# Sparse attention and a routed mixture of experts: tokens placed in their expert's rows batch by batch, outputs added by DMA

## The chip, the cores and the metric

The kernel runs on one core of a Trainium2 chip (trn2). The metric is the device time of one execution in microseconds, as a median over runs. Engine names are those of the profile: PE multiplies matrices, DVE, ACT and POOL are the vector, scalar and GpSimd engines, SP issues most of the DMAs. Indirect DMAs, whose rows are chosen by an index in on-chip memory, are issued by POOL.

## The reference

An attention over 4 batches, 8 heads, 768 positions and a head dimension of 64 comes first. Of each row only the six most promising chunks of 32 keys are attended to. Its output, 3072 tokens of width 512, goes into a dense two-layer network and, for each token, into one of eight expert networks, the one with the highest gate value:

```python
x = attn_out.transpose(0, 2, 1, 3).reshape(B * S, H * D)      # 3072 x 512
y_dense = np.maximum(x @ w1_dense, 0.0) @ w2_dense            # 512 -> 512 -> 512
logits = x @ w_gate                                           # 8 experts
expert_idx = np.argmax(logits, axis=1)
gate_w = softmax(logits)[token, expert_idx]
y_moe[mask_e] = gate_w[mask_e] * (np.maximum(x[mask_e] @ w1[e], 0.0) @ w2[e])
out = y_dense + y_moe                                         # 3072 x 512, fp32
```

## The kernel before

**Attention stage.** The 16 pairs of heads run one after another, four pairs for each batch, each in 11 units (`NU`). A unit is a score matmul (L447), an exponential on ACT (L451), for some units a mask by POOL (`affine_select`, L453), and the product with the values (L466). The scores are issued two units ahead. The outputs of a batch are collected in `xbig`, a buffer for one batch, of which there are two. Preparations of later pairs (casts on POOL, transposes, chunk bounds on DVE) are laid among the units.

**Fills.** When a batch's attention is done, `batch_fills(b)` gives a list of closures that are laid among the units of the next batch: six transposes of the tokens (`xtr`), the gate (`gate`), the ranks (`ranks`, unit 9), and the dense network, of which `l1` computes hidden activations for three token tiles and `l2` one token tile of outputs. `ranks` counts, by matmuls with triangular and all-one matrices, the position of each token among those of its expert. `digits` writes a one-hot row for each token into `Am`. `gate` stores the tokens of the batch, with their gate weight, in two DRAM tables: `xo` (1056 bytes a row) and the right part of `xd` (3104 bytes a row). `l2` stores the dense outputs in the left part of `xd`.

**Tail.** After the attention, the fills of the last batch run by themselves. From the ranks of all batches a list of 31 blocks of 128 rows is built: each expert's tokens rounded up to whole blocks, and some blocks at the end that may be empty (24 token tiles give at most 24 + 7 blocks). The list is turned round by 24 matmuls (`pm`, L606) into `gi`, the token of every row of every block, and `si`, where its output goes; rows without a token get an index out of bounds and are not written.

**Blocks.** The loop over the 31 blocks is written out by hand, so that each engine finds work of the neighbouring blocks: in iteration i PE does the first layer of block i (`e1`), transposes the tokens of block i + 1 (`tx`), does the second layer of block i - 1 (`e2`) and transposes the hidden activations of block i (`th`). The weights' addresses come from registers (`offs`), loaded from the list. POOL gathers the rows of block i + 4 in one indirect DMA from `xd` (L646, buffer `xg`, six of them; the first four blocks take their tokens from `xo`). DVE multiplies the result by the gate weight and adds the dense outputs that came with the gather (L693), and POOL scatters the sum to `out` (L694).

The framework adds the semaphores, keeps each engine's instructions in an order near that of the program, and gives a buffer to its next user once all readers and writers of the last one are done. For a DMA that is when the data have landed.

Of the kernel before, what the change touches and what calls it, by code (L numbers as in the profile page):

```python
# [17 lines left out]
def kernel(  # L18
# [26 lines left out]
    RW = 2 * Dm + XW  # L45
# [5 lines left out]

    xd = dram.tile([N, RW], U16, name="xd")

    xo = dram.tile([N, XW], U16, name="xo")
    xov = xo.rearrange("(m p) w -> p m w", p=128)
    NX = 4
    xdv = xd.rearrange("(m p) w -> p m w", p=128)
# [10 lines left out]
    mx = ctx.enter_context(tc.tile_pool(name="mx", bufs=2))  # L68

# [78 lines left out]
    eone = const.tile([128, E], FP)  # L148
    relb = const.tile([128, NM], FP)
    Am = const.tile([128, NM, 128], HF)  # L150
    ones = const.tile([128, 128], HF)
    low = const.tile([128, 128], HF)
    io128 = const.tile([128, 128], HF)
    ioblk = const.tile([128, NBLK], HF)

    num = const.tile([128, NM], FP)
    xbig = [const.tile([128, NT, XW], HF, name=f"xbig{i}") for i in range(2)]

    def route_consts():
        for x2 in xbig:  # L160
            nc.gpsimd.memset(x2[:, :, Dm:XW], 0.0)
        nc.gpsimd.iota(iom8, pattern=[[0, NT], [1, E]], base=-E, channel_multiplier=0, allow_small_or_imprecise_dtypes=True)
        nc.gpsimd.memset(osum[:, 0], 0.0)
        nc.gpsimd.memset(eone, 1.0)
        nc.gpsimd.memset(ones, 1.0)
        nc.gpsimd.memset(low, 1.0)
        nc.gpsimd.affine_select(out=low, in_=low, compare_op=ALU.is_gt, fill=0.0,
                                base=0, pattern=[[1, 128]], channel_multiplier=-1)
        nc.gpsimd.iota(io128, pattern=[[1, 128]], base=0, channel_multiplier=0, allow_small_or_imprecise_dtypes=True)
        nc.gpsimd.iota(ioblk, pattern=[[1, NBLK]], base=0, channel_multiplier=0, allow_small_or_imprecise_dtypes=True)  # L170
        half = 2048 // 128
        nc.gpsimd.iota(num[:, 0:half], pattern=[[128, half]], base=-2048, channel_multiplier=1,
                       allow_small_or_imprecise_dtypes=True)
        nc.gpsimd.iota(num[:, half:], pattern=[[128, NM - half]], base=1, channel_multiplier=1,
                       allow_small_or_imprecise_dtypes=True)
# [57 lines left out]

    def batch_fills(b):
# [12 lines left out]
        def gate():  # L247
# [20 lines left out]
            for dst in (xov, xdv[:, :, 2 * Dm :]):  # L268
                nc.sync.dma_start(out=dst[:, b * NT : (b + 1) * NT], in_=xbig[b % 2].bitcast(U16))

        def rank():

            ohb = oh[:, b * NT : (b + 1) * NT]
            rk = ptile("rk", [128, NT + 1, E], FP, "rk")
            nc.tensor.matmul(rk[:, 0:NT], low, ohb, start=True, stop=False, skip_group_check=True)
            if b:
# [7 lines left out]
            ri = mg.tile([128, NT], mybir.dt.int32, name="ri")  # L284
            with nc.allow_low_precision("whole numbers below 2**24"):
                nc.vector.tensor_reduce(out=ri, in_=rt1, op=ALU.add, axis=mybir.AxisListType.X)
            r7 = mg.tile([128, NT], mybir.dt.int32, name="r7")
            nc.vector.tensor_single_scalar(r7, ri, 127, ALU.bitwise_and)
            rb = mg.tile([128, NT], mybir.dt.int32, name="rb")
            nc.vector.tensor_single_scalar(rb, ri, 7, ALU.arith_shift_right)  # L290
            rf = mg.tile([128, NT], FP, name="rf")
            nc.vector.tensor_copy(rf, r7)
            nc.vector.tensor_copy(relb[:, b * NT : (b + 1) * NT], rb)
            return rk, rf

        def digits(rf, t):
            m = b * NT + t
            nc.vector.tensor_scalar(Am[:, m], io128, rf[:, t : t + 1], num[:, m : m + 1], ALU.is_equal, ALU.mult)

        keep = {}  # L300

        def ranks():
            _, keep["rf"] = rank()
            ohb = oh[:, b * NT : (b + 1) * NT]
            with nc.allow_low_precision("whole numbers up to 24"):
                nc.vector.tensor_reduce(out=osum[:, b + 1], in_=ohb.rearrange("p t e -> p e t"), op=ALU.add,
                                        axis=mybir.AxisListType.X)
                nc.vector.tensor_add(osum[:, b + 1], osum[:, b + 1], osum[:, b])
# [14 lines left out]
        def l2(g, i, hold):  # L323
            def f():
# [7 lines left out]
                nc.sync.dma_start(out=xdv[:, m, 0 : 2 * Dm], in_=ys.bitcast(U16))  # L332
# [17 lines left out]
        for t in range(NT):  # L350
            at.setdefault(11 + 4 * t, []).append(lambda t=t: digits(keep["rf"], t))
# [3 lines left out]
        return out_list, dense, rank, digits, at  # L355
# [202 lines left out]
    with (  # L558
# [4 lines left out]
        tc.tile_pool(name="eg", bufs=6) as eg,  # L563
# [4 lines left out]
        a, d, rank, digits, _ = batch_fills(B - 1)  # L568
        for f in a:
            f()  # L570

        def dense(n):
            for _ in range(n):
                if d:
                    d.pop(0)()


        dense(2)
        rk, rf = rank()
        cnt = rk[:, NT]  # L580
        ni = const.tile([128, E], mybir.dt.int32)
        nc.vector.tensor_single_scalar(ni, cnt, 127.0, ALU.add)
        digits(rf, 0)
        nc.vector.tensor_single_scalar(ni, ni, 7, ALU.arith_shift_right)
        digits(rf, 1)
        be = const.tile([128, E], FP)
        nc.vector.tensor_tensor_scan(be, eone, ni, 0.0, ALU.mult, ALU.add)
        digits(rf, 2)
        bs = const.tile([128, E], FP)
        nc.vector.tensor_tensor(bs, be, ni, ALU.subtract)  # L590
        digits(rf, 3)
        tb = const.tile([128, NM, E], FP)
        nc.vector.tensor_tensor(tb, oh, bs.unsqueeze(1).to_broadcast([128, NM, E]), ALU.mult)
        digits(rf, 4)
        tbr = const.tile([128, NM], FP)
        nc.vector.tensor_reduce(out=tbr, in_=tb, op=ALU.add, axis=mybir.AxisListType.X)
        digits(rf, 5)
        bf = const.tile([128, NM], HF)
        nc.vector.tensor_add(bf, tbr, relb)
        eqb = const.tile([128, NM, NBLK], HF)  # L600
        nc.vector.tensor_tensor(eqb, ioblk.unsqueeze(1).to_broadcast([128, NM, NBLK]),
                                bf.unsqueeze(2).to_broadcast([128, NM, NBLK]), ALU.is_equal)
        dense(6)
        pm = p4.tile([128, NBLK], FP, name="pm")
        for m in range(NM):
            nc.tensor.matmul(pm, Am[:, m], eqb[:, m], start=(m == 0), stop=(m == NM - 1))  # L606
        up = const.tile([128, NBLK], FP)
        nc.vector.tensor_single_scalar(up, pm, 0.0, ALU.is_gt)
        gi = const.tile([128, NBLK], mybir.dt.int32)
        nc.vector.scalar_tensor_tensor(gi, pm, 2048.0, up, ALU.add, ALU.subtract)  # L610
        em = const.tile([128, NBLK], FP)
        nc.vector.tensor_scalar(em, pm, 0.0, 8192.0, ALU.is_equal, ALU.mult)
# [135 lines left out]
```

The softmax here doesn't subtract the row's maximum and nothing guards it: scores larger than these inputs give would overflow.

## Time and profile before

| | |
|---|---|
| time, median of 3 runs | 287.54 us (287.31 to 287.95) |
| time of the profiled execution | 306.61 us |
| its span in the profile | 304.9 us |
| mean granted PE clock over the span | 0.945 |
| PE busy | 241.6 us (79%) |
| DVE busy | 196.8 us (65%) |
| ACT busy | 174.4 us (57%) |
| POOL busy | 155.4 us (51%) |
| moved by DMA | 60.73 MB |

The profiled execution is slower than the others by 19 us, so durations read in it are compared with its own time. A share of busy time is a mean over stages that differ: attention until about 174.6 us of the span, then the last batch's fills, then the blocks. A busy PE is not a PE at its peak, since matmuls are pipelined and their clock can be reduced; the granted clock is listed by stage.

### The profile page before, as it was taken

To read this page: it belongs to the slowest core of one execution; us is meant where nothing else is said; L and a number is where in the kernel's file an instruction comes from. 1 tells how busy PE (TensorE), PEld (TensorE's weight loads), DVE (VectorE), ACT (ScalarE), POOL (GpSimd) and SP (SyncE) were. 2 spreads that over 40 slices of the span, in tenths; PEclk is the share of its full clock that TensorE was granted. 3 is DMA by queue.
4 is the path that set the end of the run, shared out by engine and by line. 5 is a ranking of instruction groups with operands and counts; after the bars stand their busy time and mean duration, and the time that the engine had idled before them with its cause. 6 is when DMAs were issued, how large, how long until landed. Compare 5 with 4: busy or idle time off the path is not lost.

```text
span 304.9 us, 7337 instructions
## 1 busy us (share of the span) xinstructions
PE 241.6 (79%) x2615; PEld 153.6 (50%) x2615; DVE 196.8 (65%) x620; ACT 174.4 (57%) x325; POOL 155.4 (51%) x203
## 2 busy tenths in 40 slices
PE   1179787789999888999899898838786697779691
PEld 1156566566667665667665554413443354335250
DVE  5479999999988999979996385122333233324141
ACT  3649788785979878789688633311333333234240
POOL 6566755553655636445412104473755566737432
PEclk9999999999999999999999999785999979959688
DMA  7999999999998999999972148685555755655510
GB/s 187 275 257 217 190 257 190 210 230 307 204 296 256 221 281 220 233 208 184 154 233 105 69 167 266 163 290 184 157 161 192 222 170 184 222 171 180 190 66 1
DMA packets 75636, 60.73 MB, mean 199 GB/s; under 512 B 28942, under 2 KB 68878, under 8 KB 75600
## 3 DMA queue, kind: packets, MB, share of 16 engines
q0 software_dynamic: 15184, 28.60, 40.5%
q1 hardware_dynamic: 60416, 31.66, 38.5%
q8 instruction: 21, 0.34, 0.4%
q14 instruction: 15, 0.12, 0.1%
HBM read 50.62 MB, written 20.91 MB: 235 GB/s over the span
## 4 chain that ended last, share of the span: by engine, by line
PE 40%; DVE 26%; ACT 11%; issue 10%; POOL 5%; DMA 5%; another core or an unknown queue 1%; POOLq 1%; ACTq 0%; SPq 0%; DVEq 0%
PE yp L690 8%; PE hp L673 7%; PE sp L447 5%; PE hp L318 4%; ACT ex L451 4%; DVE ks L389 4%; PE yp L327 4%; DVE m L426 3%; DMA xd<-ys 2%; POOL out_dram L694 2%; DVE rT L436 2%; DVE xbig L477 2%; PE tp L665 2%; PE tp L682 2%; PE op L466 2%
## 5 line engine op out<-in xcount | busy, mean ns | idle before, releaser
L451 ACT ACTIVATE ex<-sp 128x512 f16<-128x512 f32 (+1 forms) x176 | 90.0, 601 | 10.3 <-PE op L466 6.3
L447 PE MATMUL sp<-rT,kT 128*128 128x128 f16 (+3 forms) x384 | 63.9, 261 | 6.6 <-ACT ex L451 3.7
L453 POOL TENSOR_SCALAR_AFFINE_SELECT ex<-ex 128x512 f16<-128x512 f16 x48 | 32.7, 688 | 44.7 <-ACT ex L451 40.3
L694 POOL DMA_INDIRECT out_dram<-yo,si x31 | 31.4, 1013 | 37.0 <-DVE yo L693 32.2
L466 PE MATMUL op<-v,ex 128*128 128x65 f16 x672 | 45.7, 193 | 2.0 <-DVE xbig L477 1.0
L667 DVE COPY exT<-tp 128x512 f16<-128x512 f16 x31 | 13.1, 424 | 52.3 <-PE tp L665 24.7
L673 PE MATMUL hp<-we,exT 128*128 x124 | 37.1, 428 | 9.7 <-DVE exT L667 5.8
L684 ACT COPY ehT<-tp 128x512 f16<-128x512 f16 x31 | 18.1, 585 | 43.3 <-PE tp L682 29.9
L466 PEld LDWEIGHTS <-ex 128*128 128x128 f16 x672 | 35.5, 97 | 13.4 <-POOL ex L453 2.8
L690 PE MATMUL yp<-we,ehT 128*128 x124 | 36.8, 424 | 6.2 <-issue 3.7
L447 PEld LDWEIGHTS <-kT 128*128 128x128 f16 x384 | 29.8, 98 | 14.4 <-issue 9.2
L646 POOL DMA_INDIRECT xg<-xd,gi x31 | 29.8, 963 | 12.4 <-issue 7.6
L676 ACT ACTIVATE eh<-hp 128x512 f16<-128x512 f32 x31 | 18.5, 597 | 28.8 <-PE hp L673 14.9
L389 DVE TENSOR_REDUCE ks<-kp 128x24 f16<-128x768 f16 x32 | 29.3, 941 | 7.9 <-ACT kp L385 7.8
L693 DVE SCALAR_TENSOR_TENSOR yo<-yp,xg 128x512 f32<-128x512 f32 x27 | 20.2, 749 | 16.0 <-PE yp L690 10.0
L318 PE MATMUL hp<-xT,wd 128*128 128x384 f16 x128 | 26.1, 324 | 2.8 <-DVE rt L283 1.3
L327 PE MATMUL yp<-wd,hT 128*128 128x512 f16 x96 | 24.6, 378 | 0.7 <-DVE ys L224 0.3
L320 ACT ACTIVATE hT<-hp 128x384 f16<-128x384 f32 x32 | 15.7, 491 | 15.8 <-PE hp L318 12.7
L370 POOL CAST k<-kf 128x768 f16<-128x768 f32 x16 | 13.2, 824 | 19.6 <-PE pp L383 16.6
L673 PEld LDWEIGHTS <-exT 128*128 128x128 f16 x124 | 12.5, 108 | 20.5 <-issue 7.8
L690 PEld LDWEIGHTS <-ehT 128*128 128x128 f16 x124 | 12.3, 107 | 16.5 <-issue 7.4
L385 ACT COPY kp<-pp 128x768 f16<-128x768 f16 x16 | 12.9, 805 | 10.2 <-PE pp L383 10.2
(128 smaller groups left out, 422.8 us busy)
## 6 DMA issues: line engine op xcount, KB each, us to landing
we<-in_moe_w_dram POOLq DMA_DIRECT2D x16, 512.0 KB
kf<-in_k_dram SPq DMA_DIRECT2D x32, 192.0 KB, 4.6
qf<-in_q_dram SPq DMA_DIRECT2D x32, 192.0 KB, 4.5
vf<-in_v_dram SPq DMA_DIRECT2D x32, 192.0 KB, 7.4
xd<-ys SPq DMA_DIRECT2D x24, 256.0 KB, 4.0
xo<-xbig SPq DMA_DIRECT2D x4, 792.0 KB, 6.4
xd<-xbig SPq DMA_DIRECT2D x4, 792.0 KB, 8.4
wd<-in_moe_w_dense_dram POOLq DMA_DIRECT2D x2, 512.0 KB
```

The source lines that it names most:

```text
L318: nc.tensor.matmul(hp, wd[:, ko, j * 128 : (j + 1) * 128], xT[:, ko, g * G * 128 : (g + 1) * G * 128], start=(ko == 0), stop=(ko == NK - 1))
L327: nc.tensor.matmul(yp, hold["h"][:, j, i * 128 : (i + 1) * 128], wd[:, NK + j], start=(j == 0), stop=(j == NK - 1))
L389: nc.vector.tensor_reduce(out=ks[:, i], in_=kp.rearrange("d (c w) -> d c w", w=32), op=op, axis=mybir.AxisListType.X)
L447: nc.tensor.matmul(sp[:, o : o + w], kT[p % NB][g][:, kt * 128 : (kt + 1) * 128], rT[p % NB][g][:, a * 128 : z * 128], start=(o == 0), sto ...
L451: nc.scalar.activation(ex[:, 0:o], sp[:, 0:o], AF.Exp, scale=0.125)
L453: nc.gpsimd.affine_select(out=ex, in_=ex, compare_op=ALU.is_ge, fill=0.0, base=0, pattern=[[0, 4], [1, 2], [2, 64]], channel_multiplier=-1)
L466: nc.tensor.matmul(s["op", g][:, t * (D + 1) : (t + 1) * (D + 1)], ex[:, o : o + 128], v16[p % NB][:, g, kt, :], start=first, stop=(last_o ...
L646: nc.gpsimd.indirect_dma_start(out=dst, out_offset=None, in_=src, in_offset=bass.IndirectOffsetOnAxis(ap=gi[:, i : i + 1], axis=0))
L673: nc.tensor.matmul(hp, s["xT"][:, ko], wef[:, bass.ds(offs[i] + ko * 512, 512)], start=(ko == 0), stop=(ko == NK - 1))
L690: nc.tensor.matmul(yp, s["hT"][:, j], wef[:, bass.ds(offs[i] + (NK + j) * 512, 512)], start=(j == 0), stop=(j == NK - 1))
L693: nc.vector.scalar_tensor_tensor(o, yp, s["x"][:, Dm : Dm + 2].bitcast(FP), s["y"], ALU.mult, ALU.add)
L694: sc = nc.gpsimd.indirect_dma_start(out=out, out_offset=bass.IndirectOffsetOnAxis(ap=si[:, i : i + 1], axis=0), in_=o, in_offset=None, bou ...
```

## The change

The tables `xo` and `xd` go, and with them the one-hot digits, the list by matmuls, and all gathers. In their place:

- One DRAM table has room for all tokens in each expert's part (`CAP` = 3200 rows for each of eight experts) and one empty block at its end. Ranks now include the expert's first row (one more matmul, `ebase`), so that they are the row in the table (`slot`).
- `place(t)` scatters the 128 tokens of one tile to their rows by an indirect DMA. It is laid at units 12, 15, ... 27 of the next batch's attention. A token's row also carries its own number in `out` (32 bits next to the gate weight).
- `lists` is called twice: after batch 2 it lists the first 11 blocks (`N1`), those that are certain to be full of tokens of the batches 0 to 2, and after batch 3 the other 20 (`N2`). It writes the first row of each block (`ro`) and its weights' address (`eo`).
- `fetch(i)` loads a block's 128 rows by a plain DMA on SP, with the address in a register of SP. Five blocks are fetched ahead (`AHEAD`), in six buffers.
- The last batch's fills, its placing and the storing of empty rows behind each expert's last token (`empty`) are laid among the first ten blocks (`extra`). Blocks 0 to 10 are declared independent of the last batch's placing.
- The dense outputs are stored in `out` itself, each tile in two DMAs of 64 rows. In `e2` DVE only multiplies by the gate weight, and the scatter to `out` adds to what is there (`compute_op=ALU.add`). Its indices lie in the fetched rows, so the row's buffer is in use until that scatter is done.

```diff
-    xd = dram.tile([N, RW], U16, name="xd")
-    xo = dram.tile([N, XW], U16, name="xo")
+    CAP = N + 128
+    EMPTY = E * CAP
+    table = dram.tile([EMPTY + 128, XW], U16, name="table")
+    N1 = (N * (B - 1) // B - E * 127 + 127) // 128
+    N2 = NBLK - N1
+    outv = out.rearrange("(m p j) d -> m j p d", p=64, j=2)
...
-            for dst in (xov, xdv[:, :, 2 * Dm :]):
-                nc.sync.dma_start(out=dst[:, b * NT : (b + 1) * NT], in_=xbig[b % 2].bitcast(U16))
+            nc.gpsimd.tensor_copy(xbig[b % 2][:, :, Dm + 2 : Dm + 4].bitcast(mybir.dt.int32), num[:, b * NT : (b + 1) * NT])
...
+        def place(t):
+            def f():
+                sc = nc.gpsimd.indirect_dma_start(
+                    out=table, out_offset=bass.IndirectOffsetOnAxis(ap=keep["slot"][:, t : t + 1], axis=0),
+                    in_=xbig[b % 2][:, t].bitcast(U16), in_offset=None)
+                apart(sc, "rows", "every token has a row of its own")
+                if b == B - 1:
+                    tc.declare_no_dep(sc.ins, group="full", reason="the first blocks were full before this batch")
+            return f
...
-                nc.sync.dma_start(out=xdv[:, m, 0 : 2 * Dm], in_=ys.bitcast(U16))
+                for j in range(NJ):
+                    st_ = nc.sync.dma_start(out=outv[m, j], in_=ys[64 * j : 64 * j + 64])
...
-            at.setdefault(11 + 4 * t, []).append(lambda t=t: digits(keep["rf"], t))
+            at.setdefault(12 + 3 * t, []).append(place(t))
...
+        def fetch(i):
+            es[i]["x"] = xg = eg.tile([128, XW], U16, name="xg")
+            ld = nc.sync.dma_start(out=xg, in_=table[bass.ds(rows[i], 128)])
+            if i < N1:
+                tc.add_to_no_dep_group("full", ld.ins)
...
-            o = eg.tile([128, Dm], FP, name="yo")
-            nc.vector.scalar_tensor_tensor(o, yp, s["x"][:, Dm : Dm + 2].bitcast(FP), s["y"], ALU.mult, ALU.add)
-            sc = nc.gpsimd.indirect_dma_start(out=out, out_offset=bass.IndirectOffsetOnAxis(ap=si[:, i : i + 1], axis=0),
-                                         in_=o, in_offset=None, bounds_check=N - 1, oob_is_err=False)
+            o = et.tile([128, Dm], FP, name="yo", bufs=4)
+            nc.vector.tensor_scalar(o, yp, s["x"][:, Dm : Dm + 2].bitcast(FP), None, ALU.mult)
+            sc = nc.gpsimd.indirect_dma_start(
+                out=out, out_offset=bass.IndirectOffsetOnAxis(ap=s["x"][:, Dm + 2 : Dm + 4].bitcast(mybir.dt.int32), axis=0),
+                in_=o, in_offset=None, bounds_check=N - 1, oob_is_err=False, compute_op=ALU.add)
...
+        AHEAD = 5
+        load_rows(N1)
+        for i in range(AHEAD):
+            fetch(i)
+        load_offs(N1)
         tx(0)
+        extra = {0: a[:NT], 1: [a[NT], ranks], 2: places[:3], 3: places[3:], 4: [empty]}
+        for n, f in enumerate(d):
+            extra.setdefault(2 + n * (N1 - 3) // len(d), []).append(f)
         for i in range(NBLK):
+            if i + AHEAD == N1:
+                load_rows(NBLK)
+            if i + 1 == N1:
+                load_offs(NBLK)
+            if i + AHEAD < NBLK:
+                fetch(i + AHEAD)
             e1(i)
...
             if i + 1 < NBLK:
                 tx(i + 1)
+            for f in extra.get(i, ()):
+                f()
             if i > 0:
                 e2(i - 1)
             th(i)
```

## The prediction

> **What bounds the kernel now.** I read the busy table over time first, cut where the work changes: attention ends with the last use of its buffers at about 174.6 us, the routing of batch 3 follows, and from 189 us on the 31 expert blocks run. The columns are busy us (instructions) of PE, weight loads, DVE, ACT and POOL, then the granted clock, the DMA share and GB/s.
>
> ```profile
> 174.60:186.00 11.40, 10.76 (x115) 6.46 (x115) 10.04 (x46) 4.39 (x10) 0.00 (x0) 1.00 0.64 219
> 186.00:196.00 10.00, 8.00 (x42) 3.67 (x40) 2.08 (x5) 3.61 (x7) 5.41 (x6) 0.84 0.57 168
> 196.00:210.00 14.00, 7.88 (x42) 3.93 (x41) 3.01 (x5) 2.95 (x5) 8.80 (x10) 0.74 0.82 256
> 200.00:285.00 85.00, 63.33 (x382) 33.01 (x380) 27.14 (x47) 28.21 (x48) 50.73 (x52) 0.88 0.60 192
> 0.00:174.60 174.60, 143.35 (x1991) 102.38 (x1992) 150.30 (x512) 131.59 (x251) 90.28 (x137) 1.00 0.98 217
> ```
>
> Until 186 us PE is full. From 186 to 210 it is busy 15.9 of 24 us, much of it at a reduced clock. The chain of waits says why: the dense outputs must land in DRAM before a block's rows can be gathered from the same table.
>
> ```profile
> 184.79 3.47 DMA xd<-ys
> 189.77 3.68 DMA xd<-ys
> 199.21 5.15 DMA xg<-xd,gi
> ```
>
> Then the steady part. The costliest groups show two POOL instructions for each block, and the timeline shows how they follow one another:
>
> ```profile
> L694 POOL DMA_INDIRECT out_dram<-yo,si x31 | 31.4, 1013 | 37.0 <-DVE yo L693 32.2
> L646 POOL DMA_INDIRECT xg<-xd,gi x31 | 29.8, 963 | 12.4 <-issue 7.6
> ```
> ```profile
> 225.35 0.97 POOL L646 DMA_INDIRECT xg<-xd,gi  x1 [0.30 <-PE yp L690]
> 225.40 1.03 PE L673 MATMUL hp<-we,exT 128*128 x4
> 226.62 1.02 POOL L694 DMA_INDIRECT out_dram<-yo,si  x1 [0.30 <-issue]
> 227.57 1.03 PE L673 MATMUL hp<-we,exT 128*128 x4
> 227.94 0.97 POOL L646 DMA_INDIRECT xg<-xd,gi  x1 [0.30 <-issue]
> ```
>
> PE at full clock repeats every 2.17 us (225.40 to 227.57). POOL needs 0.97 + 0.30 + 1.02 + 0.30 = 2.59 us for a block. So **POOL is the slower of the two**, PE idles, and PE's clock falls. Measured: 25 scatters begin between 200 and 285 us, 3.4 us a block; PE is busy 63.3 of 85 us at a mean clock of 0.88.
>
> **What the Trainium skill says.** (1) "DMA: Bandwidth & Descriptors", section "SWDGE vs HWDGE vs iDMA": an accumulating DMA can only be issued from GpSimd. So the scatter stays on POOL; only the gather can leave. No accumulate is in this trace. (2) "Collectives: The Full Stack", section "The bandwidth ceiling": a reducing DMA is slower than a copy because it needs two source reads, about half the rate, not because of the addition. Not shown here either; I use a factor of 2. (3) The first page again, section "Two DMAs through the same engine are not ordered": of two read-modify-write packets directly after one another the second mostly read stale data. So such packets overlap in an engine, and a row isn't waited for before the next begins. (4) "TensorE: Matmul & The Clock Gate", section "What's actually happening": the clock halves after an idle window of some 3.4 us and returns after a busy one. The trace agrees: four L690 matmuls take 1.02 us at best, 1.91 us at 205 us, right after a PE idle of 4.5 us.
>
> **The change, part by part.** The profiled execution took 306.61 us (span 304.9, 1.7 around it), 19.1 us over the median of 287.54. I sum against the profiled one, then carry over.
>
> *Attention stage.* Off DVE: 18 digit masks at 312 ns (5.6 us), and 12 small casts and shifts at about 164 ns (2.0 us). Onto DVE: the first block list, 15 small instructions, some 11 at 0.17 and 4 at 0.3 us by the rows of be, ni, ge and ef: 3.1 us. Net -4.5 us on an engine busy 150.3 of 174.6 us, so part of it could shorten the stage. Onto POOL: 18 row scatters. The nearest row, L646, gives 0.97 + 0.30 us each, 22.9 us on an engine busy 90.3 of 174.6. They stand in POOL's order ahead of the mask selects that PE waits for:
>
> ```profile
> POOL ex L453 <- ACT ex L451: 40.3, 27, 7.4
> PEld L466 <- POOL ex L453: 2.8, 6, 1.0
> ```
>
> POOL waits 40.3 us for the exponentials, PE only 2.8 us for POOL, so most scatters find a gap. Bounds: -4.5 us (DVE all on the path) to +6 us (18 times a third of a microsecond lost behind a scatter; all of it lost is a rival). I take 0. SP issues 18 more stores (0.33 us each) and 6 big ones fewer; SP only waits here, and its waiting instructions hold back loads made two head pairs ahead, so nothing. One more rank matmul per batch (0.19 us): nothing.
>
> *Between attention and experts.* Gone: rank digits, the tb/eqb/pm chain, the 24 pm matmuls (0.76 us), the gathers xo and the wait for the dense stores. The first 11 blocks need only batches 0 to 2, whose rows were placed during attention; SP can fetch five of them ahead. PE work in this stage at full clock: 24 transposes (6 x 0.22 = 1.3), gate 0.8, ranks 0.4, eight L318 groups at 0.82 (6.6) and six L327 groups at 0.86 (5.2): 14.3 us. All of it now lies between expert blocks. Start (first transpose, its copy, register loads; the copy alone is 0.42 us, and PE waited 1.5 us at 190.97): 2 us.
>
> *Blocks.* PE 31 x 2.17 = 67.3 us. POOL falls to one instruction: 1.02 + 0.30 = 1.32 us, with 0.5 us more if three instead of two descriptors must be written; even 1.8 us is under 2.17. Six row scatters add 7.6 us once, in iterations that dense work stretches to about 3.6 us. SP takes the fetches, 0.33 us each: covered. The DVE output step loses an operand: nothing. The second list (16 small DVE instructions, about 3.4 us) stands ahead of a block's exT copy: I charge 2 us of PE.
>
> **The new wait** is in the fetch. A fetch needs the row buffer of the block six before it, which is free only when that block's accumulating scatter has landed. With T the time of a block: its e2 starts 1.08 us into the next iteration; from e2's start to the end of the scatter's instruction the last blocks took 3.08 us (294.40 to 297.48); a plain indirect transfer lands 1.85 us after its instruction (first xo gather: ends 187.19, PE has it at 189.04), with a doubled transfer I estimate 2 to 3; SP and the fetch's landing 2.5 (the shortest store landed in 2.0). That is 9.2 at the middle, and the rows are wanted 0.86 us into the iteration four later: 4T = 8.3, T = 2.1 us. Just inside 2.17, so I take PE's pace; each microsecond of landing more costs 0.25 us a block. Queued behind a waiting fetch on SP: dense stores (three ys buffers, whose copies on DVE and ACT would wait), the zero rows and the row registers. The dense stores come three at a time, some four iterations apart, and a fetch holds SP up for two to three: no charge.
>
> *End.* From the last e2's start to the end of the span:
>
> ```profile
> 298.54 1.02 PE L690 MATMUL yp<-we,ehT 128*128 x4 [0.82 <-ACT ehT L684]
> 300.63 0.98 POOL L694 DMA_INDIRECT out_dram<-yo,si  x1 [1.08 <-DVE yo L693]
> ```
>
> 304.9 - 298.5 - 0.9 for the group itself = 5.5 us, unchanged.
>
> **Sum.** Tail = 2 + 14.3 + 67.3 + 2 + 5.5 = 91 us against 130.3 in the profile. Of the 21.7 us in which PE stood idle between 200 and 285, several pauses stop ACT, DVE and PE together with no releaser shown; I leave 8 us of them. Profile: 174.6 + 91 + 8 + 1.7 = 275, 31 below 306.6. The unprofiled runs have at most 287.5 - 1.7 - 174.6 = 111 us of tail, so less to lose: 174.6 + 91 + 1.7 + 2 for clock and buffers = **269 us**, 18.5 below the median.
>
> **Rivals.** *Ring of row buffers* (0.22): an accumulating landing 2 us longer than assumed gives T = 2.6 to 2.7, as slow as POOL was; 20 blocks x 0.5 = 10, so 279 us. For it: the margin above is nil. *No overlap* (0.05): the first fetches still wait for batch 3; then the 8 us hole of 186 to 210 stays, 277 us. *Slower: the accumulate itself* (0.13). If rows of one engine are added one after another with a trip to DRAM each, eight rows an engine at 0.5 us are 4 us a block: 20 x 1.8 = 37 us more, 306. It turns the sign from T = 3.1 us on (269 + 20 x 0.93 = 287.5), which is a landing about 4 us longer than assumed. Against it: item (3). *Slower: placing during attention* (0.04): all 22.9 us of POOL on the path gives 292.
>
> **How the numbers follow.** PE's pace 0.56 (own range 260 to 275), ring 0.22, no overlap 0.05, the two slower cases 0.17. Faster by over 0.2% (about what measurement can tell from no change): 0.82; same 0.01; slower 0.17. The range 259 to 286 holds the faster cases and leaves out the slower.
>
> **What would show it.** Right: no idle of PE over 2 us between 175 and 200, e1 groups 2.2 us apart after block 11, one POOL instruction a block, clock 0.95 or more. Ring: PE or its loads wait for xg's DMA with SP behind the scatter. Accumulate: scatter packets several times the length of a copy. Placing: PE's wait for POOL selects well over 2.8 us, attention ending after 180. Attention ending before 170 would say DVE was the bound there and 269 too high.

## The result, and the profile after

The changed kernel takes **305.07 us** (median of 4 runs, 303.67 to 308.63) beside 287.43 us for the kernel before: a ratio of 1.060 (95% interval 1.054 to 1.066). In two later comparisons on two chips, each beside fresh runs of the kernel before, it was 1.041 (1.031 to 1.051) and 1.042 (1.028 to 1.056). Ratios here and below leave out executions more than 1.5% above the fastest of their kernel, so they can differ by up to 0.007 from the quotient of the medians. The forecast was 269 us; the change costs 12 to 18 us where it was to save 18.5.

The profiled execution took 304.44 us, its span is 302.7. The busy table over time of the changed kernel, cut as in the prediction (busy us (instructions) of PE, weight loads, DVE, ACT, POOL, then clock, DMA share, GB/s):

```profile
0.00:175.80 175.80, 141.59 (x1966) 102.58 (x1967) 143.05 (x495) 131.09 (x249) 108.59 (x163) 0.98 0.96 205
...
186.00:196.00 10.00, 9.62 (x97) 6.19 (x96) 7.36 (x31) 4.98 (x10) 3.80 (x4) 0.93 0.24 40
196.00:210.00 14.00, 9.36 (x59) 4.63 (x57) 4.49 (x7) 4.90 (x9) 9.90 (x8) 0.92 0.87 197
...
200.00:285.00 85.00, 62.52 (x387) 32.73 (x386) 26.97 (x46) 29.26 (x51) 37.40 (x25) 0.87 0.67 126
```

The last line is the one to compare: PE is busy 62.5 of 85 us, no more than before (63.3), although POOL fell from 50.7 to 37.4 us and is no bound any more. The profile of before was taken in an execution of 306.61 us; in one of 287.79 us (b_again, below) PE even reached 68.7:

```profile
200.00:285.00 85.00, 68.73 (x448) 34.82 (x447) 33.99 (x57) 33.10 (x56) 56.74 (x58) 0.90 0.63 208
```

Something else holds PE. The costliest groups show the parts as they were planned: one POOL instruction a block and 24 placing ones. The scatter, now adding, takes 1556 ns where the plain one took 1013:

```profile
L694 POOL DMA_INDIRECT out_dram<-yo,xg x31 | 48.2, 1556 | 69.8 <-DVE yo L693 51.6
...
L366 POOL DMA_INDIRECT table<-xbig,slot x24 | 23.5, 979 | 12.9 <-issue 5.8
...
L665 PE MATMUL tp<-ident,xg 128*128 128x128 f16 x124 | 13.0, 234 | 15.6 <-DMA xg<-table 15.6
```

The waits after 176 us (what waited, for what, us in total, times, longest) name two causes for PE and, in the SP queue, what stands behind the first:

```profile
PE tp L665 <- DMA xg<-table: 15.6, 5, 5.8
PE hp L673 <- issue: 6.9, 1, 6.9
```
```profile
SPq L657 <- DMA out_dram<-yo,xg: 77.4, 24, 16.4
SPq L762 <- DMA out_dram<-yo,xg: 12.2, 3, 8.4
SPq L641 <- DVE yo L693: 4.3, 1, 4.3
```

SP spends 77 us waiting to fetch a block's rows (L657) until an earlier block's scatter, which reads its indices from the same buffer, has landed. The other hole, 6.9 us in one piece, has no releaser. PE's timeline shows both kinds, three of the holes:

```profile
211.16 0.61 PE L665 MATMUL tp<-ident,xg 128*128 128x128 f16 x4 [5.79 <-DMA xg<-table]
...
235.18 1.44 PE L673 MATMUL hp<-we,exT 128*128 x3 [6.92 <-issue]
...
249.41 0.61 PE L665 MATMUL tp<-ident,xg 128*128 128x128 f16 x4 [2.87 <-DMA xg<-table]
```

The hole before 235.18 belongs to no data: in the trace PE's own queue runs one register load there, the 20 weight addresses of the second list, from 227.7 on for 7.28 us. It is the longer one of the two loads in this view of the list's tile (minimum, median and maximum in ns):

```profile
L641 PEldq TENSOR_LOAD <-eo x2: 1758/4521/7284, 179.4 to 227.7; - x2
```

In attention, the waits for POOL's masks, to be compared with 40.3 and 2.8 before:

```profile
POOL ex L521 <- ACT ex L519: 31.6, 25, 3.5
...
PEld L534 <- POOL ex L521: 8.1, 8, 2.5
```

The end of the span is as forecast: the last second-layer group starts at 296.31, and 302.7 - 296.3 - 0.9 = 5.5 us.

### The profile page after: what moved, and what is told of

The parts are those of the page before. It is cut to its first block, busy times and chain, and to the rows that moved or that the text cites. A ratio compares the mean times of both kernels' runs of the same rounds, so it can differ in the third digit from the quotient of the medians.

```text
span 302.7 us, 7430 instructions
## 1 busy us (share of the span) xinstructions
PE 236.5 (78%) x2595; PEld 153.8 (51%) x2595; DVE 188.8 (62%) x592; ACT 174.7 (58%) x325; POOL 162.6 (54%) x200
## 3 DMA queue, kind: packets, MB, share of 16 engines
q1 hardware_dynamic: 60288, 30.58, 40.2%
## 4 chain that ended last, share of the span: by engine, by line
PE 27%; issue 24%; POOL 22%; DVE 12%; ACT 10%; DMA 3%; POOLq 1%; SPq 0%; ACTq 0%; DVEq 0%
POOL out_dram L694 13%; PE sp L515 7%; ACT ex L519 4%; PE yp L391 4%; POOL table L366 4%; PE hp L382 4%; PE op L534 3%; PE pp L488 2%; DVE ks L457 2%; DVE m L494 2%; POOL ex L521 2%; PE pp L502 1%; PE tp L262 1%; PE hp L673 1%; DMA kf<-in_k_dram 1%
## 5 line engine op out<-in xcount | busy, mean ns | idle before, releaser
L519 ACT ACTIVATE ex<-sp 128x512 f16<-128x512 f32 (+1 forms) x176 | 91.1, 602 | 17.3 <-PE sp L515 10.7
L694 POOL DMA_INDIRECT out_dram<-yo,xg x31 | 48.2, 1556 | 69.8 <-DVE yo L693 51.6
L534 PEld LDWEIGHTS <-ex 128*128 128x128 f16 x672 | 36.2, 99 | 18.7 <-POOL ex L521 8.1
L673 PE MATMUL hp<-we,exT 128*128 x124 | 36.8, 420 | 9.3 <-issue 6.9
L693 DVE TENSOR_SCALAR yo<-yp,xg 128x512 f32<-128x512 f32 x31 | 23.2, 749 | 23.4 <-PE yp L690 23.3
L457 DVE TENSOR_REDUCE ks<-kp 128x24 f16<-128x768 f16 x32 | 29.2, 945 | 12.5 <-ACT kp L453 12.4
L690 PE MATMUL yp<-we,ehT 128*128 x124 | 34.7, 406 | 0.8 <-ACT ehT L684 0.8
L676 ACT ACTIVATE eh<-hp 128x512 f16<-128x512 f32 x31 | 18.5, 597 | 25.7 <-PE hp L673 25.4
L366 POOL DMA_INDIRECT table<-xbig,slot x24 | 23.5, 979 | 12.9 <-issue 5.8
L382 PE MATMUL hp<-xT,wd 128*128 128x384 f16 x128 | 27.7, 347 | 1.9 <-DVE rt L305 1.0
L665 PE MATMUL tp<-ident,xg 128*128 128x128 f16 x124 | 13.0, 234 | 15.6 <-DMA xg<-table 15.6
L665 PEld LDWEIGHTS <-xg 128*128 128x128 f16 x124 | 9.8, 105 | 24.5 <-DMA xg<-table 18.0
L673 PEld LDWEIGHTS <-exT 128*128 128x128 f16 x124 | 11.7, 105 | 17.8 <-issue 11.4
```

The source lines that it names most:

```text
L366: sc = nc.gpsimd.indirect_dma_start(out=table, out_offset=bass.IndirectOffsetOnAxis(ap=keep["slot"][:, t : t + 1], axis=0), in_=xbig[b % 2 ...
L382: nc.tensor.matmul(hp, wd[:, ko, j * 128 : (j + 1) * 128], xT[:, ko, g * G * 128 : (g + 1) * G * 128], start=(ko == 0), stop=(ko == NK - 1))
L457: nc.vector.tensor_reduce(out=ks[:, i], in_=kp.rearrange("d (c w) -> d c w", w=32), op=op, axis=mybir.AxisListType.X)
L519: nc.scalar.activation(ex[:, 0:o], sp[:, 0:o], AF.Exp, scale=0.125)
L534: nc.tensor.matmul(s["op", g][:, t * (D + 1) : (t + 1) * (D + 1)], ex[:, o : o + 128], v16[p % NB][:, g, kt, :], start=first, stop=(last_o ...
L673: nc.tensor.matmul(hp, s["xT"][:, ko], wef[:, bass.ds(offs[i] + ko * 512, 512)], start=(ko == 0), stop=(ko == NK - 1))
```

## The experiments

"Before" is the kernel before, run on the same chip beside them. Chips differ: the same kernel took about 287 us in the first comparison and on two chips after it, and 303 to 305 on two others. So only ratios are compared from one chip to another.

| run | edit to the changed kernel | us | before | ratio (95%) |
|---|---|---|---|---|
| b_again | (the kernel before) | 287.77 | 287.65 | 1.001 (0.999 to 1.004) |
| a_again | none | 299.54 | 287.65 | 1.041 (1.031 to 1.051) |
| e1_ring12 | 12 row buffers | 299.02 | 303.42 | 0.979 (0.970 to 0.988) |
| e2_plain | scatter without the add | 296.71 | 303.42 | 0.976 (0.969 to 0.983) |
| e3_offs4 | PE registers in fours | 302.58 | 303.42 | 0.993 (0.989 to 0.996) |
| g1_after | none | 318.95 | 304.87 | 1.042 (1.028 to 1.056) |
| g2_ring12 | 12 row buffers | 301.08 | 304.87 | 0.984 (0.975 to 0.994) |
| g3_offs4 | PE registers in fours | 308.04 | 304.87 | 1.006 (1.002 to 1.010) |
| g4_own_tile | 12 buffers, own tile for the PE list | 291.44 | 304.87 | 0.955 (0.947 to 0.962) |
| h1_shifted | the same, list 44 bytes into it | 281.99 | 286.32 | 0.985 (0.977 to 0.994) |
| c1_ring_offs | 12 buffers, PE registers in fours | 278.62 | 287.65 | 0.973 (0.966 to 0.979) |
| c2_parts | the same for SP too, 4 at the start | 276.12 | 287.22 | 0.964 (0.959 to 0.970) |
| h2_own_tiles | 12 buffers, own tiles for both lists | 272.95 | 286.32 | 0.950 (0.942 to 0.958) |
| f1_cut_noplace | ends after attention, no placing | 178.80 | 287.22 | |
| f2_cut_after | ends after attention | 183.54 | 287.22 | |
| f3_cut_before | the kernel before, ends there | 180.27 | 287.22 | |
| e4_cut_after | as f2 | 194.57 | 303.42 | |
| e5_cut_before | as f3 | 180.33 | 287.65 | |

**Theory**: the new wait in the fetch (six row buffers) and the register loads, both priced at next to nothing, hold PE. **Rivals**: the accumulate is slow by itself; the placing costs attention its gain.

### Both kernels again on one chip

b_again:

> The kernel before, unchanged, profiled beside the others on one chip. Its runs of the first comparison took 287 us and those of the second 303, so its trace is needed from the same chip as the experiments'. If chips differ in the attention stage alone: attention ends later than 172.6 us by as much as the whole is longer than 287. If the difference lies in the blocks: the tail after attention is longer instead.

a_again:

> The changed kernel, unchanged, on the same chip as the kernel before. If 6% is its true cost: about 1.06 times the kernel before. If the first comparison had the two on chips of different speed: between 0.99 and 1.02 times. Theory A (ring) expects the last 20 blocks to take 3 us each in either case.

Measured: 287.77 and 299.54 us. A profiled execution of the kernel before took 287.79 us here, so the profile itself costs nothing. In the first profiled one, of 306.61 us, attention's last product starts at 172.6 us as it does here; its 19 us more all lie behind that (132.3 us to the end of the span, 113.5 here). Whether a slower chip made them isn't shown: no trace of the kernel before was taken on one, and the changed kernel loses most of its time there in attention (last product at 189.1 us in g1_after, 175.8 in a_again). The blocks of b_again (first-layer groups, L673) follow at 2.54 us on the mean from the sixth on, (276.7 - 213.1)/25, close to POOL's 2.59 us as read in the prediction.

Attention's last product starts at 172.6 us in b_again and 175.8 in a_again; from there to the end of the span it is 113.5 and 121.1 us. So 3.2 us of the loss lie in attention and 7.6 after it.

### The ring of row buffers

Only the number of buffers, and only the add:

```diff
-    eg = ctx.enter_context(tc.tile_pool(name="eg", bufs=6))
+    eg = ctx.enter_context(tc.tile_pool(name="eg", bufs=12))
```

> One edit to the changed kernel: 12 row buffers (xg) instead of 6, still five fetched ahead. Theory A, the ring: the last 20 blocks take 3.1 us each because a fetch waits for the scatter six blocks earlier to land (4.5 to 5.4 us after its issue) and then lands itself only 4.4 us later. With 12 buffers neither wait is on the path; blocks go to about 2.2 us, 20 x 0.9 = 18 us less, some of the 5.8 us hole at 205 us goes too: 280 to 288 us against 305. Theory B, the accumulate's own rate: the engines that move the data can't add 128 rows in less than about 3 us; then the scatters only pile up and the time stays within 1% of 305.

```diff
-                in_=o, in_offset=None, bounds_check=N - 1, oob_is_err=False, compute_op=ALU.add)
+                in_=o, in_offset=None, bounds_check=N - 1, oob_is_err=False)
```

> One edit to the changed kernel: the last scatter overwrites instead of adding, so the dense outputs are left out of the result. Six row buffers as before. Theory A: the scatter's instruction falls from 1.55 to 1.02 us and its landing by some 1 to 1.5 us; each takes a quarter of its length off the ring, 4T falls from 12.4 to about 10.4, T from 3.1 to 2.6: 20 x 0.5 = 10 us less, 293 to 297. Theory B: the rate of adding is all of it, blocks go to 2.2 us and the time to 285 or less.

Measured: 299.02 and 296.71 us where the kernel before takes 303.42. The changed kernel itself was not run on this chip; at 1.04 times the kernel before it would take some 316. In both the blocks after the register load follow at 2.17 us, PE's pace (two of e2's at about 2.3). First-layer groups of e2_plain:

```profile
258.09 1.03 PE L673 MATMUL hp<-we,exT 128*128 x4
260.27 1.03 PE L673 MATMUL hp<-we,exT 128*128 x4
```

With six buffers and a plain scatter (985 ns) the ring turns fast enough. This run alone doesn't decide: theory A expected 2.6 us a block here, and 2.2 is what the rival B expected. The run with twelve buffers decides: its scatters add, take 1550 ns as before, and its blocks follow at 2.17 us all the same. So the add slows the kernel only through the buffer that its landing keeps busy. SP's waits for it fall from 77.4 us to 29.3 (e1) and 53.6 (e2), which no longer reach PE. The second run on a chip with the changed kernel beside it:

> Twelve row buffers in place of six, nothing else. Theory (the ring of row buffers and the queue behind its waits cost some two thirds of the loss): 19 blocks from 2.91 to 2.17 us give 14 us and SP's late first fetch 3 to 6 us, so 280 to 286 beside a changed kernel at 299.5, the single slow load of 20 PE registers still there as a hole of 6 to 7 us. Rival (the register load is the larger part, the ring only fills time that the pause behind it leaves): 290 to 294.

> The changed kernel again, so that the single edits beside it are compared with it on one chip. Where the kernel before takes about 287.5 us it should take 299 to 305 (ratio 1.040 to 1.062). A chip on which the kernel before takes 303 should give about 316.

g1_after 318.95, g2_ring12 301.08: the ring is worth 17.9 us there, 5.8 points of the ratio. The rival for g2, that the register load is the larger part, would have needed 290 to 294 beside a changed kernel at 299.5, a gain of 6 to 9 us; it falls. All of the gain lies in blocks 11 to 30 (60.4 us from start to start in g1, 42.6 in g2).

How the ring turns can be followed in a_again. POOL starts the scatter of block 16; SP, behind it, can issue the fetch of block 22 into the same buffer; PE gets the rows:

```profile
256.43 1.55 POOL L694 DMA_INDIRECT out_dram<-yo,xg  x1 [0.62 <-DVE yo L693]
```
```profile
261.56 0.33 SPq L657 DMA_DIRECT2D xg<-table  x1
```
```profile
265.79 0.40 PE L665 MATMUL tp<-ident,xg 128*128 128x128 f16 x4 [1.46 <-DMA xg<-table]
```

5.13 us from the scatter to the fetch, 4.23 us from there to the transposes. Over the scatters of blocks 5 to 24 the first step's median is 4.8 us. It is 4.8 in e3_offs4 too, which adds, and 3.1 in e2_plain, which doesn't, on one chip. The second step took 3.1 to 5.1 us in the four places after 240 us where PE waited more than a microsecond. PE's pace is uneven: the first-layer groups of blocks 12 to 15, 17 to 20, 22 to 25 and 27 to 30 follow at 2.17 us, and the waits lie between these fours.

The largest ring hole of a_again, 6.05 us, has a second ingredient. POOL's queue around it, DVE's output step of block 1, and SP's queue:

```profile
186.99 1.63 POOL L694 DMA_INDIRECT out_dram<-yo,xg  x1 [14.46 <-DVE nb L325]
188.92 0.98 POOL L366 DMA_INDIRECT table<-xbig,slot  x1 [0.30 <-DVE eo L351]
...
195.26 0.96 POOL L366 DMA_INDIRECT table<-xbig,slot  x1 [0.30 <-issue]
196.53 1.61 POOL L694 DMA_INDIRECT out_dram<-yo,xg  x1 [0.30 <-issue]
```
```profile
189.66 0.73 DVE L693 TENSOR_SCALAR yo<-yp,xg 128x512 f32<-128x512 f32 x1
```
```profile
192.03 0.34 SPq L657 DMA_DIRECT2D xg<-table  x1
193.18 4.11 SPq L708 DMA_DIRECT2D table<-zt  x7
201.60 0.35 SPq L657 DMA_DIRECT2D xg<-table  x1
```
```profile
207.11 0.61 PE L665 MATMUL tp<-ident,xg 128*128 128x128 f16 x4 [6.05 <-DMA xg<-table]
```

The six placing scatters of the last batch stand between the scatters of blocks 0 and 1, so block 1's starts only at 196.53, although DVE had its rows ready at 190.39 (189.66 + 0.73). Its landing lets the fetch of block 7 go at 201.60, and PE, which was ready at 201.06, gets the rows at 207.11. With twelve buffers this hole is gone, placing and all: on the same chip the period of block 6, from the start of its first-layer group to that of the next, falls from 12.0 to 3.5 us (c1_ring_offs). No run moved the placing, so its part is read from the order of the queues and not shown by an experiment. On the two slower chips PE has a hole of 4 to 6 us two or three blocks earlier instead, with twelve buffers too (5.6 us in g1 and g2, put down to "DVE ys"), and block 6 takes 3.5 us.

### The register loads

The second list's weight addresses, 20 registers of PE, four at a time:

```diff
-            if i + 1 == N1:
-                load_offs(NBLK)
+            if i + 1 >= N1 and len(offs) <= i + 1 and len(offs) < NBLK:
+                load_offs(min(len(offs) + 4, NBLK))
```

> One edit to the changed kernel: the weights' addresses of the last 20 blocks are loaded into PE's registers four at a time, over five blocks, instead of all 20 ahead of block 10's matmuls. In the trace the single load of 20 took 7.3 us and PE stood for 6.9 us. If the cost goes by the number of registers and is on the path: the hole is split in five of about 1.4 us, which fall partly into ring waits that PE has anyway: 3 to 6 us less. If PE has the ring's waits behind it in any case, the hole only moves: no change within 1%.

> Six row buffers as in the changed kernel; only the second list's weight addresses are loaded into PE's registers four at a time. Theory (ring first): while the ring holds the blocks at 2.9 us, a saved pause is given back in the ring, since the scatters and fetches went on during it; 0 to 3 us saved, 296 to 300 beside 299.5. Rival (the pause counts in full): 292 to 294.

Measured: 302.58 us (before 303.42) and 308.04 (before 304.87, unchanged kernel 318.95). So loading in fours alone saves 10.9 us there, 3.6 points of the ratio with some 1.5 points of uncertainty. My expectation for g3, that the ring would give a saved pause back (0 to 3 us saved), was wrong; the hole itself was 6.0 us in g1. The blocks behind it are shorter too (from the start of block 11 to that of block 30, 60.4 us in g1 and 55.1 in g3); behind its pause of 7.4 us the first layer takes 1.87 us in a_again instead of 1.03. A load of four takes about 1.0 us, the first of them 2.3 in g3.

Why is the load slow, when the kernel before loaded 27 registers, from 16 bytes into their tile, in 2.73 us?

```profile
L634 PEldq TENSOR_LOAD <-eo x2: 752/1742/2733, 190.1 to 206.0; - x2
```

In the changed kernel it starts at the twelfth number of a tile of 31, 44 bytes in. g4_own_tile gives the second list a tile of its own; h1_shifted puts 11 unused numbers in front of it there:

```diff
-    eo = const.tile([1, NBLK], mybir.dt.int32)
+    eos = [const.tile([1, N1], mybir.dt.int32, name="eo1"), const.tile([1, N2], mybir.dt.int32, name="eo2")]
...
```

> Twelve row buffers, and the second list's 20 weight addresses in a small tile of their own, loaded in one instruction as before. If the slow load (6 to 8 us for 20 registers, 2.7 us for 27 in the kernel before) came from an address in the middle of a tile that is not a round number of bytes, it falls to about 2 to 3 us and the time is 4 to 5 us below that of twelve buffers alone. If it comes from the number of registers and what else the core does in that moment, it stays at 5 to 8 us and the time is within 1.5 us of it.

```diff
-    eos = [const.tile([1, N1], mybir.dt.int32, name="eo1"), const.tile([1, N2], mybir.dt.int32, name="eo2")]
+    eos = [const.tile([1, N1], mybir.dt.int32, name="eo1"), const.tile([1, NBLK], mybir.dt.int32, name="eo2")]
...
-            nc.vector.tensor_scalar(eos[last], ef, float(E - 1), float(2 * NK * 512), ALU.min, ALU.mult)
+            nc.vector.tensor_scalar(eos[last][:, i0 : i0 + n], ef, float(E - 1), float(2 * NK * 512), ALU.min, ALU.mult)
...
```

> As the run with the second list's weight addresses in a tile of their own, but that tile has 11 unused numbers in front, so the load of 20 registers begins 44 bytes into it again. If the place of the first byte makes the load slow, it takes 6 to 8 us again and the ratio to the kernel before is that of twelve buffers alone (0.984), or 0.97 where the before takes 287 us. If sharing a tile with the first list made it slow, it stays at 1.4 us and the ratio is 0.955.

The tile view of the list (minimum/median/maximum of the two loads; the longer is that of 20 in the first and third) in g2_ring12, g4_own_tile and h1_shifted:

```profile
L641 PEldq TENSOR_LOAD <-eo x2: 1671/4322/6974, 192.6 to 240.2; - x2
```
```profile
L641 PEldq TENSOR_LOAD <-eo x2: 1375/1532/1690, 192.2 to 237.5; - x2
```
```profile
L641 PEldq TENSOR_LOAD <-eo x2: 1684/4461/7238, 179.3 to 220.3; - x2
```

6.97 us, 1.38 us, and 7.24 us again when the first number lies 44 bytes into a tile of its own (h2_own_tiles, below, on the chip of h1: 1.79 us from the first byte). So **the byte at which the load begins** decides, not the sharing of a tile. The number of registers alone doesn't explain it either: 11 from a tile's start took 1.7 us, 20 took 1.4. Only these few starts were tried (0, 16 and 44 bytes for the long loads), so where the step lies is open. g4 is 9.6 us faster than g2, more than the 4 to 5 expected; 7.0 of it lie in the periods of blocks 10 and 11 (8.95 and 3.53 us against 3.35 and 2.17). h1's ratio of 0.985 is above the 0.97 expected: PE stood 6.3 us for the load, and 2.7 us more for rows whose fetch was behind SP's own load of 20 registers. When PE loads them, the numbers have long been there: DVE wrote them at 204.9 us in g2, the load starts at 240.2.

### Both causes taken away

c1_ring_offs joins the two edits above; c2_parts also loads SP's row addresses in fours and four PE registers at the start; h2_own_tiles loads each of the second lists whole, from tiles of their own, on both engines, and four and then seven of PE's first eleven:

```diff
-    ro = const.tile([1, NBLK], mybir.dt.int32)
+    ros = [const.tile([1, N1], mybir.dt.int32, name="ro1"), const.tile([1, N2], mybir.dt.int32, name="ro2")]
...
-        load_offs(N1)
+        load_offs(4)
...
+            if i == 1:
+                load_offs(N1)
```

> Two edits to the changed kernel together: 12 row buffers and the weights' addresses loaded four at a time. Singly they gave about 299.0 and 302.6 us on a chip where the kernel before took 303.4. Theory A: with the ring open, the load of 20 registers is the next thing PE waits for, so the edits add up, and a bit more: 4 to 9 us below the ring edit alone. If the hole is covered by waits that remain: no lower than the ring edit alone.

> The changed kernel with 12 row buffers and all registers loaded in parts of four, just ahead of their use: PE's (4 at the start instead of 11) and SP's for the last 20 blocks. Against the version with 12 buffers and PE's parts alone (278.6 us, 0.9725 of the kernel before on its chip): the gap of 2.8 us before block 11, in which a fetch stood behind SP's load of 20 registers (7.7 us), should go, and some 1 us at the start: 0.955 to 0.965 of the kernel before. If the fetch was late for another reason: 0.97.

> Twelve row buffers, own tiles for the second list's weight addresses (PE) and row addresses (SP), four PE registers at the start and seven more in the second iteration. If the place of the first byte counts on SP too, SP's load of 20 falls from 5 us to 1 to 2 us. Theory: blocks at 2.17 us with no pause before the eleventh, and the time is 4 us or so below that of loading in fours everywhere: ratio 0.945 to 0.955. Rival (SP's and PE's loads were already covered there): 0.960 to 0.965.

Measured: 278.62, 276.12 and **272.95 us**, ratios 0.973, 0.964 and 0.950. All three beat both kernels. The intervals of h2 and c2, from two chips, just fail to meet (0.942 to 0.958 against 0.959 to 0.970). The two savings don't add up: 5.8 and 3.6 points singly, but 6.8 in c1 (0.973 against 1.041). c1 was expected 4 to 9 us below twelve buffers alone and is 2 to 3 below, within the intervals. Loading in fours has its own price: with PE otherwise at 2.17 us a block, the four blocks of c1 with a later load take 3.0 to 3.2. SP's load of 20 row addresses took 7.25 us in h1 and 2.92 in h2, less of a fall than expected; in c1, where it took 7.65, PE stood 2.8 us before block 11 for rows whose fetch was behind it. c2, which also loads SP's in parts, has no such stop, as expected. In h2's busy table PE is full from block 11 on, at full clock, and SP's wait for the scatters is small:

```profile
220.00:264.00 44.00, 43.35 (x316) 24.25 (x315) 22.34 (x39) 23.05 (x39) 30.55 (x20) 1.00 0.88 152
```
```profile
SPq L659 <- DMA out_dram<-yo,xg: 16.6, 9, 4.0
```

### Attention with and without the placing

Kernels that end after the attention stage, with no experts and the last batch's fills left out; f1 also leaves out the 18 placing scatters:

```diff
-        for t in range(NT):
-            at.setdefault(12 + 3 * t, []).append(place(t))
```

> The changed kernel cut at the same place, without the 18 row scatters of the batches 0 to 2 (so the table is left empty). If the scatters hold up POOL's mask selects: the 3 us go and the stage ends at or, with DVE 4.5 us lighter than before, up to 3 us below the cut kernel before. If something else costs the 3 us (more stores, the copy of the token numbers, the lists): no change against the changed kernel's cut.

> The changed kernel cut at the same place. The prediction put the stage's change at 0, between -4.5 and +6 us. The traces of both whole kernels on one chip had the last product with the values at 172.6 and 175.8 us: expected 3 us more than the cut kernel before. At 0 or less, the 3 us of those traces were chance.

> The kernel before ended when the attention stage is done, beside the next two on one chip; nothing of the last batch's routing and no block runs, and of the output only 128 x 128 is written. It took 180.3 us on the chip of the second job. It is the base for the other two cuts.

Measured: 178.80, 183.54 and 180.27 us. The placing costs 4.7 us; all else in the change saves 1.5; together 3.3 us lost. The waits for the masks, of f1 and of f2:

```profile
POOL ex L521 <- ACT ex L519: 44.4, 27, 6.7
...
PEld L534 <- POOL ex L521: 2.4, 6, 0.6
```
```profile
POOL ex L523 <- ACT ex L521: 31.9, 24, 3.5
...
PEld L536 <- POOL ex L523: 8.0, 8, 2.4
```

With the scatters, 12.5 us of POOL's waiting are filled up, and PE waits 5.6 us more for masks. That the masks stand behind the scatters in POOL's queue is the reading of these lines; the runs show that the scatters cost the time. Two first runs of such cuts:

> The changed kernel ended when the attention stage is done: nothing of the last batch's routing, no blocks; only the first 128 x 128 of the output is written. It prices the stage without the profile's effect. By its trace the stage ends at 178 us, by that of the kernel before at 174.6. With some 5 us of end around it: 181 to 185 us, 2 to 4 us more than the kernel before cut at the same place. If the 18 row scatters on POOL cost more than the trace shows: over 188.

> The kernel before ended when the attention stage is done; no routing of the last batch, no blocks, and only 128 x 128 of the output written. Beside the changed kernel cut at the same place (194.6 us on the other job's chip): 190 to 193 if placing costs 2 to 4 us of attention, as the two first traces suggest (172.6 against 177.6 for the last product with the values); 194 or more if it costs nothing and the traces only show two chips.

They took 194.57 and 180.33 us, but on different chips (before 303.42 and 287.65), so their difference says nothing; f2 and f3 are the pair on one chip.

## Why the prediction was wrong

Against 269 us stands the profiled a_again with 298.6: 29.6 us more. Put beside h2_own_tiles, which does the same work without the two causes on another chip of 287 us, nearly all of it is found. Periods are between the starts of first-layer groups. Attention's last product is the start of the last product with the values; the prediction's cut at 174.6 us lay 2.0 us behind it, which are added to its tail of 91 + 2.

| | predicted | a_again | h2_own_tiles |
|---|---|---|---|
| attention's last product | 172.6 | 175.8 | 177.7 |
| from there to the end of the span | 95 | 121.1 | 93.7 |
| period of block 6 (six placing scatters ahead) | about 3.6 | 12.0 | 3.5 |
| period of block 10 (load of 20 registers) | | 9.7 | 3.8 |
| blocks 11 to 30, start to start | 19 x 2.17 = 41.2 | 55.2 | 41.3 |

The three rows at the bottom differ from h2 by 8.5, 6.0 and 13.9 us, some 28 in all. The tail was forecast 26 us too short, attention 3.2.

- **The ring, the failed step.** "T = 2.1 us. Just inside 2.17" rested on two estimates. From the scatter's start to the fetch it put 1.02 + 2.5 = 3.5 us, and 4.8 was measured; the fetch's landing it put at 2.5, and about 4.4 was measured (median of the four above, where PE waited; the median landing of all fetches after 230 us is 3.0). Of the first 1.3 us, 0.5 is the scatter's longer instruction (1.55 us), which the prediction allowed for on POOL and left out here. Both landings were taken low: a plain factor of 2 on the 1.85 us of an indirect landing would have been 3.7, and the 2.0 us behind the 2.5 was the shortest store, where the median in the same profile was 4.0 for twice the bytes. 3.2 us more around the ring make 0.8 us a block by the prediction's own rule of 0.25, so T = 2.9; measured 55.2/19 = 2.9. That the tenths agree is in part luck: the pace is uneven, and other traces have 2.6 (e3_offs4) to 3.2 (g1). Both terms were too small, and a margin of 0.07 us was taken as "inside". The rival *ring of row buffers* named the mechanism at 0.22 but priced 2 us more and no more. The Trainium skill ("Collectives: The Full Stack", section "The bandwidth ceiling"), which the prediction used for its factor of 2, speaks of the reduce step of a collective: about half the rate of a copy, for two source reads. For this scatter the time from the end of the scatter's instruction to the fetch went from 3.1 - 0.98 = 2.1 us to 4.8 - 1.55 = 3.3, one and a half times (e2_plain against e3_offs4 and a_again).
- **SP and POOL queues, priced at nothing.** "No charge" for what stands behind a waiting fetch, and 7.6 us of placing scatters spread over long iterations: in fact these six hold the scatter of block 1, that one holds the fetch of block 7, and PE stands 6.05 us. A cost that is covered on its own engine was passed on through the ring.
- **The register load, left out.** The prediction counted register loads only at the start. The kernel before loaded 27 of the 31 at 206 us, between blocks 3 and 4, in 2.73 us, and PE stood 1.3 us there. The change moves 20 of them between blocks 10 and 11 and to a byte where the load takes 7 us, and PE stands about as long.
- **Attention at 0.** Measured +3.3 us, inside the bounds of -4.5 to +6. Both parts are there, a saving of 1.5 and a cost of 4.7; the reason given for zero ("most scatters find a gap") held for most of the 22.9 us of scatters, not for all. The rival *placing during attention* (all 22.9 us on the path) was far too high.
- **Right**: POOL as the bound before (2.54 us a block on the mean, 2.59 read), PE's 14.3 us for the last batch and 2 for the second list (h2's first eleven periods take 40.2 us, 16.3 more than eleven of 2.17), its pace of 2.17, the half microsecond that it allowed for a longer scatter instruction, the start (2.4 us of hole; 2 forecast) and the end of 5.5. Together they are the tail of 93.7 us that h2 shows, where 95 was forecast.
- **The slower rival.** *The accumulate itself* gave 306 us, close to the result for a reason that did not hold: with twelve buffers the same accumulates cost nothing (g2 and h2 run at 2.17). Nor was its turning point, T = 3.1, what made a_again slower than the kernel before: its T is 2.9, and the register load and the first hole took the rest. In the first trace and in g1 the blocks took 3.1 and 3.2 us, but by the ring.
- **The chip.** The profile of before was taken in an execution of 306.61 us; the tail read in it, 130.3 us from the cut on, is 111.5 by the same cut in an execution of 287.79 us (113.5 less 2.0). The prediction carried this over as "at most 111", and that held to half a microsecond.

Open: why the first comparison gave 1.060 and two later ones 1.041 and 1.042. In that trace the tail is 302.7 - 177.6 = 125.1 us against 121.1 in a_again, with the same holes, somewhat longer. Which part of the ring's 13.9 us in a_again is the start after the pause was not separated. Open too: what made the first profiled execution of the kernel before slower.

## What to carry to other kernels

Where a buffer is kept until a DMA lands, write the whole loop out (issue, landing, next fetch, landing, use) with landings measured in the busy stage, divide by the number of blocks that pass meanwhile (four here, with six buffers), and take a margin of nothing as a stall; twice the buffers cost one number and gave 18 of 319 us here. Ask of every instruction put into an in-order queue whose buffer the ones behind it will free. And place each list that is loaded into registers at the start of a tile of its own; loading it in parts helped less here (0.964 against 0.950).

## What the runs showed of the hardware

- A load of 20 registers took 1.4 to 1.8 us from the first byte of a tile and 6.1 to 7.7 us from byte 44 on PE; on SP 2.9 us and 4.3 to 7.7 us.
- A scatter of 128 rows of 512 fp32 numbers that adds takes 1.55 us of POOL, a plain one 0.98, and it frees the buffer with its indices about 1.7 us later (4.8 instead of 3.1 us from its start; e3_offs4 and e2_plain, one chip).
- The same program took 286 to 288 us on two chips and 303 to 305 on two others. On one of the slower two the first expert block of the run with twelve buffers starts at 194.5 us instead of 181.2 (h1, another chip, same work up to there), and 5.6 us follow in which PE waits (a "DVE ys" wait that the other chip doesn't show). Differences of a few per cent are only to be had on one chip.
